# Gated attention and a squared-ReLU layer on one core: twelve units' loads, with and without waits in the SP queue

## The chip, the core and the metric

The kernel runs on one core of a Trainium2 chip. The core has five engines, each with its own instruction stream: TensorE (PE) for matmuls, VectorE (DVE), ScalarE (ACT), GpSimd (POOL), and SyncE (SP), which here does nothing but issue transfers. Engines wait for each other and for transfers through semaphores. Every engine works strictly in its written order: an instruction that waits holds up everything behind it on the same engine. The metric is device microseconds of one execution, and smaller is better.

## What is computed

```python
def _attn_ref(q, k, v, alpha):                       # batch 4, 8 heads, 768 tokens, 48 wide
    for t in range(S):
        state = alpha[:, :, t, :, None] * state + np.einsum('bhd,bhe->bhde', k[:, :, t], v[:, :, t])
        y[:, :, t] = np.einsum('bhd,bhde->bhe', q[:, :, t], state)

def _moe_ref(x, w_in, w_out):                        # 3072 tokens, 384 -> 2048 -> 384
    h = x @ w_in
    r = np.maximum(h, 0.0)
    g = r * r
    return (g @ w_out)
```

A gated linear attention runs over the tokens, and its output, with the heads side by side, goes through two dense layers with a squared ReLU between them.

## The kernel before

The work is cut into 12 units of 256 tokens: three steps along the sequence for each of four batch rows, all rows at one step first. A unit goes through these parts (the line numbers are those of the profile of before):

- **Loads.** Four transfers of 384 KB each, alpha, k, q and v, into one of four raw buffers (line 526, function `load`). Unit g uses buffer g modulo 4. Units 1 and 2 are loaded by POOL, all the others by SP.
- **Front.** From alpha come the decays: a product of pairs on DVE or POOL (lines 633, 635), logarithms on ACT (636, 675), a cumulative sum as a matmul on PE (642), exponentials on ACT (653, 655, 679). DVE multiplies them into k (709) and q (704). ACT or POOL casts v (700, 699).
- **Transposes.** From unit 3 on, two DMA transposes, a "pair" below, which SP issues (line 720), bring keys and queries into the buffer kqt.
- **Scores, output, state.** PE computes the scores (898), DVE masks them (909), PE computes the output of the attention and the new state (790, 801, 769), and ACT or DVE copies the output out as xbf (929, 931).
- **Dense layers.** xbf is transposed to xt, from unit 4 on by one DMA transpose that SP issues (line 950). PE multiplies with the first weight (1000), ACT or DVE applies the ReLU (1008, 1010), the square follows (1018, 1021, 1022), PE multiplies with the second weight (1040), ACT or DVE evicts to osb (1047, 1049), and SP issues the store (1056).

Nobody writes the engines' orders by hand. Every step is handed to `add` of a small planner (class `Program`) with an engine, a cost, a priority and what it reads and writes. `schedule` plays the whole program through with these costs and so fixes the order on each engine. `fill` puts dummy matmuls into the early holes of PE. `place` works out which semaphore waits each instruction needs, given what its engine has already waited for, and `emit` writes them. A step's dependencies are in `deps`, and `schedule` and `place` both read them.

Some dependencies do not come from data. `load` gives them through the argument `after`: the load that `AFTER` names (for every unit from 4 on the queries of the unit ahead, `(g - 1, "q")`, which for unit 4 are those of unit 3), and from unit 5 on a step of the unit ahead that `BEHIND` names: the logarithm `ln` for alpha, the multiplication `ekm` for k, the first transpose `tr0_` for q and v. These are called pacing waits here. In SP's queue, units interleave in this way from unit 5 on (the number is the unit): alpha 6, k 6, pair 5, transpose to xt 4, q 6, v 6, store, alpha 7, k 7, pair 6, transpose to xt 5, q 7, v 7, store, and so on.

Of the kernel before, what the change touches and what calls it, by code (L numbers as in the profile page):

```python
# [14 lines left out]
class Op:  # L15


    __slots__ = ("alts", "eng", "fn", "cost", "prio", "deps", "idx", "lag", "sem", "start", "end", "pos", "name",
                 "users", "ndeps", "mode", "ready", "land")

    def __init__(self, alts, prio, name):
        self.alts, self.prio, self.name = alts, prio, name
        self.eng = self.fn = self.cost = None
        self.deps = {}
        self.lag = 0
        self.sem = None
        self.users = []
        self.pos = None
        self.mode = ("F", "F")
        self.ready = 0.0  # L30
        self.start = self.end = self.land = None


class Program:
# [37 lines left out]
    def add(self, eng, fn, cost, prio, reads=(), writes=(), name="", dma=None, lag=0, after=(), mode=("F", "F"),  # L72
            alts=None):

        reads, writes = ([h for k in keys for h in ((k + (0,), k + (1,)) if len(k) == self.HALVED.get(k[0]) else (k,))]
                         for keys in (reads, writes))
        choices = {eng: (fn, cost)}
        if alts:
            choices.update(alts)
        if name in self.CHOSEN:  # L80
            choices = {self.CHOSEN[name]: choices[self.CHOSEN[name]]}
        op = Op(choices, prio + self.MOVED.get(name, 0), name)
        op.idx = len(self.ops)
        op.lag = lag
        op.mode = mode
        if dma is not None:
            if dma not in self.dma_sems:
                self.dma_sems[dma] = self.nc.alloc_semaphore("d_" + dma)
                self.dma_count[dma] = 0
            self.dma_count[dma] += 1  # L90
            op.sem = (dma, self.dma_count[dma])
        for o in after:
            op.deps[o] = True
        for k in reads:
            w = self.writer.get(k)
            if w is not None:
                op.deps[w] = True
            if k[0] == "ps":
                for r in self.readers.get(k, ()):
                    op.deps.setdefault(r, False)  # L100
        for k in writes:
            w = self.writer.get(k)
            if w is not None:
                op.deps[w] = True
            for r in self.readers.get(k, ()):
                if r is not op:
                    op.deps.setdefault(r, False)
        for k in reads:
            self.readers.setdefault(k, []).append(op)
        for k in writes:  # L110
            self.writer[k] = op
            self.readers[k] = []
        op.deps.pop(op, None)
        self.ops.append(op)
        return op
# [113 lines left out]
    def fill(self, make, sizes, until, after, cold):  # L229
# [23 lines left out]
            o.pos = i  # L253
        self.order["pe"] = new

    def place(self):
        known = {}
        snap = {}
        waits = {}
        seq = sorted(self.ops, key=lambda o: (o.start, o.idx))  # L260
        needed = set()

        def stream(o):
            return ("dma", o.sem[0]) if o.sem is not None else ("eng", o.eng)

        def place_of(o):
            return o.sem[1] if o.sem is not None else o.pos + 1

        for o in seq:
            kn = known.setdefault(o.eng, {})  # L270
            want = {}
            for d, raw in o.deps.items():
                if d.sem is None and d.eng == o.eng == "pe":
                    continue
                s, p = stream(d), place_of(d)
                if kn.get(s, 0) >= p:
                    continue
                if s not in want or place_of(want[s]) < p:
                    want[s] = d
            mine = []  # L280
            for d in sorted(want.values(), key=lambda d: -d.start):
                s, p = stream(d), place_of(d)
                if kn.get(s, 0) >= p:
                    continue
                mine.append(d)
                needed.add(d)
                for s2, p2 in snap[d].items():
                    if kn.get(s2, 0) < p2:
                        kn[s2] = p2
                if kn.get(s, 0) < p:  # L290
                    kn[s] = p
            waits[o] = mine
            snap[o] = dict(kn)
        self.waits = waits
        self.value = {}
        for ops in self.order.values():
            n = 0
            for o in ops:
                if o.sem is not None:
                    self.value[o] = 16 * o.sem[1]  # L300
                elif o in needed:
                    n += 1
                    self.value[o] = n
        self.needed = needed
# [34 lines left out]
def pe_ns(count, cols, at_once=1):  # L339
    return count * max(cols / 2.4 + 2.5, 25) / at_once  # L340
# [6 lines left out]
def dve_ns(n, rate=1.0):  # L347
    return 150 + n / 0.96 / rate
# [6 lines left out]
def bass_gla_recurrent__then__act_relu_squared_kernel(  # L355
# [24 lines left out]
    DENSE = {0: 19172, 1: 35978, 2: 46351, 3: 61182, 11: 160500}  # L380
    POOL_LOADS = {1: "akqv", 2: "akqv"}
    RATIO = 4
    NRAW, NQKS, NKQT, NPM, NV, NXT, NGT, NRR, NOSB = 4, 3, 3, 2, 4, 4, 2, 4, 2
    WS = 2
    LATE_STATE = (1, 2)
# [48 lines left out]
    pr = Program(nc)  # L434
# [18 lines left out]
    for i in range(2):  # L453
        add("dve", fill(LAF[i][:, :, :, D:64].rearrange("p j h d -> p (j h) d"), 0.0), 250, -1e6 - 10,
            writes=[("laf", i)])
        add("dve", fill(LAB[i][:, :, D:64], 0.0), 150, -1e6 + 20, writes=[("lab", i)])
    for i in range(NQKS):
        add("dve", fill(QKS[i][:, :, :, :, D:64].rearrange("p a j h d -> p (a j h) d"), 0.0), 500, -1e6 + 10,
            writes=[("qks", i, 0), ("qks", i, 1)])
# [7 lines left out]
    for part in (OWN[0:64, 0:H:2], OWN[64:128, 1:H:2]):  # L467
# [3 lines left out]
        writes=[("ident",)])  # L471
# [29 lines left out]
    load_op = {}  # L501
# [4 lines left out]
    def named(x):  # L506
        return next(o for o in pr.ops if o.name == x)

    BEHIND = {"a": "ln", "k": "ekm", "q": "tr0_", "v": "tr0_"}

    def load(g):
        b, i = units[g]
        t0 = i * T
        p0 = g * P
        r, la, qs, kt, pm, vb, x2 = (g % n for n in (NRAW, 2, NQKS, NKQT, NPM, NV, 2))
        first, last = i == 0, i == NST - 1
        sr, sw = 2 * b + i % 2, 2 * b + (i + 1) % 2

        for j, t, nm in ((0, alpha, "a"), (1, k, "k"), (2, q, "q"), (3, v, "v")):
            src = t[b, :, t0:t0 + T, :].rearrange("h (p j) d -> p h (j d)", j=2)  # L520
            dst, key = RAW[r][:, j], ("raw", r, j)
            ring, cost, gate = "sp", 600, AFTER.get((g, nm), AFTER.get(g))
            if nm in POOL_LOADS.get(g, ""):
                ring, cost = "pool", 930
            dst = dst.rearrange("p h j d -> p h (j d)")
            load_op[g, nm] = add(ring, lambda e, dst=dst, src=src: e.dma_start(dst, src), cost, (L_PRIO[g] + j if ring == "sp" else W_PRIO[2] + 10 * g + j if g > 1 else -6e5 + j),  # L526
                writes=[key], name=f"ld{nm}{g}", dma=f"{nm}{r}{ring}", lag=1230 if ring == "sp" else 1130,
                after=([load_op[gate]] if gate else []) + ([named(f"{BEHIND[nm]}{g - 1}")] if g >= 5 else []))

    def front_by_heads(g, p0):  # L530

# [96 lines left out]
    def decays_by_pair(g, p0, r, la, last):  # L628
# [11 lines left out]
        def m1(incl):  # L640
            def run(pe):
                ins = pe.matmul(psW[:, 0:HD], (LINC if incl else LSTR)[:], LAB[la][:, :, 0:D])  # L642
                if incl and not last:
                    for p in range(NPR):
                        ins = pe.matmul(psW[:, HD + 2 * p:HD + 2 * p + 2],
                                        LAB[la][:, 2 * p:2 * p + 2, :].rearrange("p h d -> p (h d)"), ONES2[:],
                                        start=(p == 0), stop=True, skip_group_check=True)
                return ins
            return run
# [7 lines left out]
        if not last:  # L657
# [5 lines left out]
                          dve_ns(HD))})  # L663
        if g < RATIO:
            add("pe", m1(False), pe_ns(1, HD), p0 + 530, reads=[("lab", la), ("lstr",)], writes=[("ps", "W")],
# [397 lines left out]
    for g in range(3, G):  # L1063
# [3 lines left out]
             ("wout", 1): (2, "k"), 3: ("wout", 0)}  # L1067
    AFTER.update({g: (g - 1, "q") for g in range(4, G)})
    load(0)
    load(1)  # L1070
    for w in range(WS):
        weight(0, w)
    load(2)
    for w in range(WS):
        weight(1, w)
    for st in ORDER:
        kind, g = st[0], int(st[1:])
# [10 lines left out]
        else:  # L1088
# [4 lines left out]
    pr.schedule()  # L1093
    pr.fill(lambda n: lambda pe: pe.matmul(psO[:, 0:n], ZERO[:, 0:128], ZERO[:, 0:n], skip_group_check=True),  # L1094
            ((512, 216, 420), (256, 109, 250)), min(o.start for o in pr.order["pe"] if o.name.startswith("s1_")), zero, 4600)
    pr.place()
    pr.emit()

# [27 lines left out]
```

## Time and profile before

| | us |
|---|---|
| median of 3 runs | 176.74 |
| lowest and highest run | 175.2, 177.66 |
| span of the profiled execution | 178.0 |
| PE busy in it | 168.6 |
| ACT busy in it | 119.4 |
| DVE busy in it | 120.3 |

The profile is one recorded execution. Its times are counted from the start of its span. A timeline row has the start, the length, the engine, the source line, the operation, the tile written and the tile read, and how many instructions were merged. In square brackets stands how long the engine was idle before the row and what ended that idle time. SP's rows (SPq) give how long SP itself was held by issuing, not how long the transfer took. The chain of waits has rows "DMA x<-y", whose length runs from the issue to the landing of a transfer.

### The profile page before, as it was taken

To read this page: it belongs to the slowest core of one execution; us is meant where nothing else is said; L and a number is where in the kernel's file an instruction comes from. 1 tells how busy PE (TensorE), PEld (TensorE's weight loads), DVE (VectorE), ACT (ScalarE), POOL (GpSimd) and SP (SyncE) were. 2 spreads that over 40 slices of the span, in tenths; PEclk is the share of its full clock that TensorE was granted. 3 is DMA by queue.
4 is the path that set the end of the run, shared out by engine and by line. 5 is a ranking of instruction groups with operands and counts; after the bars stand their busy time and mean duration, and the time that the engine had idled before them with its cause. 6 is when DMAs were issued, how large, how long until landed. Compare 5 with 4: busy or idle time off the path is not lost.

```text
span 178.0 us, 5087 instructions
## 1 busy us (share of the span) xinstructions
PE 168.6 (95%) x2232; PEld 130.6 (73%) x2234; DVE 120.3 (68%) x194; ACT 119.4 (67%) x214; POOL 24.2 (14%) x32
## 2 busy tenths in 40 slices
PE   7998998999996999999779999999999999999994
PEld 2655787856875778787558878878778787788773
DVE  5478579789885679984838876967958835423230
ACT  3838787867828588696388759859579554566450
POOL 3920951020304224200000000000000000000000
DMA  5999999979999799998999897999999692040022
GB/s 142 344 283 204 250 271 219 243 188 232 295 218 170 206 228 127 280 216 137 290 210 165 203 242 176 243 176 206 251 215 181 146 186 41 0 133 4 0 88 88
DMA packets 71030, 33.36 MB, mean 187 GB/s; under 512 B 67552, under 2 KB 67808, under 8 KB 71008
## 3 DMA queue, kind: packets, MB, share of 16 engines
q1 hardware_dynamic: 69024, 26.75, 67.6%
q0 software_dynamic: 1984, 6.29, 14.9%
q8 instruction: 17, 0.28, 0.6%
q14 instruction: 5, 0.04, 0.1%
HBM read 25.17 MB, written 4.72 MB: 168 GB/s over the span
## 4 chain that ended last, share of the span: by engine, by line
PE 74%; DMA 15%; ACT 5%; POOL 2%; DVE 1%; issue 1%; SPq 1%
PE psWH L1000 32%; PE psO L1040 29%; DMA raw<-in_v_dram 10%; DMA raw<-in_alpha_dram 5%; PE psZ L769 2%; PE psX L801 2%; POOL raw L526 2%; PE psX L898 2%; PE psX L790 2%; PE psX L970 1%; ACT rr L1008 1%; PE psZ L898 1%; PE psWH L642 1%; ACT vbf L700 1%; PE psZ L732 1%
## 5 line engine op out<-in xcount | busy, mean ns | idle before, releaser
L1000 PE MATMUL psWH<-xt,win 128*128 128x256 bf16 x576 | 73.9, 275 | 2.9 <-ACT rr L1008 1.8
L1000 PEld LDWEIGHTS psWH<-xt,win 128*128 128x128 bf16 x576 | 65.3, 145 | 8.1 <-ACT rr L1008 2.5
L1040 PE MATMUL psO<-wout,gt 128*128 128x384 bf16 x368 | 68.9, 326 | 1.9 <-ACT osb L1047 1.9
L1008 ACT ACTIVATE rr<-psWH 128x512 bf16<-128x512 f32 x85 | 50.1, 595 | 20.3 <-PE psWH L1000 18.6
L1040 PEld LDWEIGHTS psO<-wout,gt 128*128 128x128 bf16 x368 | 34.7, 98 | 20.5 <-ACT osb L1047 2.2
L1018 DVE TENSOR_TENSOR gt<-rr 128x1024 bf16<-128x1024 bf16 (+1 forms) x39 | 24.1, 622 | 25.3 <-ACT rr L1008 25.2
L909 DVE TENSOR_TENSOR pm<-psZ,caus 128x1024 bf16<-128x1024 f32 x12 | 14.6, 1219 | 2.4 <-PE psZ L898 2.4
L1022 ACT ACTIVATE gt<-rr 128x1024 bf16<-128x1024 bf16 (+1 forms) x18 | 15.2, 843 | 0.4
L909 DVE TENSOR_TENSOR pm<-psX,caus 128x1024 bf16<-128x1024 f32 x12 | 14.6, 1219 | 1.1 <-PE psZ L898 1.1
L929 ACT ACTIVATE xbf<-psX 128x768 bf16<-128x768 f32 x11 | 8.9, 809 | 7.1 <-PE psX L790 6.4
L700 ACT ACTIVATE vbf<-raw 128x768 bf16<-128x768 f32 x9 | 7.6, 841 | 8.6 <-DMA raw<-in_v_dram 8.6
L1047 ACT ACTIVATE osb<-psO 128x384 f32<-128x384 f32 x17 | 8.3, 489 | 5.2 <-PE psO L1040 4.8
L704 DVE TENSOR_TENSOR qks<-raw,eq 128x384 bf16<-128x384 f32 x18 | 9.8, 575 | 2.5 <-DMA raw<-in_q_dram 2.3
L1094 PE MATMUL psO<-zero 128*128 128x512 bf16 (+1 forms) x32 | 9.9, 437 | 1.5 <-DVE zero L447 1.3
L709 DVE TENSOR_TENSOR qks<-raw,ek 128x768 bf16<-128x768 f32 x11 | 10.5, 952 | 0.5 <-ACT ek L621 0.4
L1010 DVE TENSOR_SCALAR rr<-psWH 128x512 bf16<-128x512 f32 x11 | 7.6, 689 | 1.7 <-PE psWH L1000 1.2
L662 DVE TENSOR_TENSOR ek<-ek,raw 128x384 f32<-128x384 f32 x9 | 6.3, 705 | 1.4 <-ACT ek L653 1.4
L864 DVE TENSOR_TENSOR smd<-psZ,sbd 128x384 bf16<-128x384 f32 x8 | 4.4, 556 | 3.9 <-PE psX L790 3.9
L635 POOL TENSOR_TENSOR prd<-raw 128x384 f32<-128x384 f32 x4 | 4.0, 1002 | 19.5 <-DMA raw<-in_alpha_dram 19.5
L1094 PEld LDWEIGHTS psO<-zero 128*128 128x128 bf16 x34 | 3.2, 110 | 4.5 <-issue 1.9
L675 ACT ACTIVATE la<-raw 128x384 f32<-128x384 f32 x8 | 4.1, 518 | 3.4 <-DMA raw<-in_alpha_dram 3.2
L636 ACT ACTIVATE lab<-prd 128x384 bf16<-128x384 f32 x10 | 5.2, 521 | 1.7 <-DVE prd L633 1.7
(118 smaller groups left out, 171.7 us busy)
## 6 DMA issues: line engine op xcount, KB each, us to landing
out_dram<-osb SPq DMA_DIRECT2D x11, 384.0 KB, 4.1
raw<-in_alpha_dram SPq DMA_DIRECT2D x10, 384.0 KB, 3.6
raw<-in_k_dram SPq DMA_DIRECT2D x10, 384.0 KB, 5.3
raw<-in_q_dram SPq DMA_DIRECT2D x10, 384.0 KB, 3.9
raw<-in_v_dram SPq DMA_DIRECT2D x10, 384.0 KB, 5.2
win<-in_moe_w_in_dram POOLq DMA_DIRECT2D x2, 768.0 KB, 10.9
wout<-in_moe_w_out_dram POOLq DMA_DIRECT2D x2, 768.0 KB, 9.0
raw<-in_alpha_dram POOLq DMA_DIRECT2D x2, 384.0 KB, 4.6
```

Of the source, the lines that this page charges most:

```text
L700: name=f"vc{g}", alts={"act": (lambda e: e.activation(vout, vin, AF.Copy), act_ns(2 * HD))})
L704: add("dve", lambda e, j=j, dst=dst: e.tensor_tensor(dst, RAW[r][:, 2, :, j, :].rearrange("p (n x) d -> p n x d", x=2), EQ[la][:, j].rearr ...
L709: add("dve", lambda e, a=a, E=E: e.tensor_tensor(QKS[qs][:, a, :, :, 0:D], RAW[r][:, 1 + a].rearrange("p h j d -> p j h d"), E[la][:].rear ...
L909: add("dve", lambda e, hf=hf, psT=psT: e.tensor_tensor(PM[pm][:, hf].rearrange("p r n j t -> p (r n) (j t)"), psT[:, :, :].rearrange("p r ...
L929: add("act", lambda e: e.activation(XBF[x2][:], psX[:, :, 0:HD], AF.Copy), act_ns(2 * HD), p0 + 6100, reads=[("ps", "X", 0), ("ps", "X", 1 ...
L1000: ins = pe.matmul(psH[hb][:, i * T:(i + 1) * T], WIN[:, kk, hidden(fj)], mov, start=(kk == 0), stop=(kk == KT - 1))
L1008: add("act", lambda e, hb=hb, rr=rr: e.activation(rr, psH[hb], AF.Relu), act_ns(512), pu + 600, reads=[("ps", "H", hb)], writes=[("rr", rb ...
L1018: add("dve", lambda e, dst=dst, sq=sq: e.tensor_tensor(dst, sq, sq, ALU.mult), 148 + k * 267, pu + 1200, reads=[("rr", rb, h) for h in ran ...
L1022: "act": (lambda e, dst=dst, sq=sq: e.activation(dst, sq, AF.Square), act_ns(k * 512))})
L1040: ins = pe.matmul(psS, GT[gt][:, fj, j, :], WOUT[:, fj, :], start=(fj == 0), stop=(fj == FT - 1))
L1047: add("act", lambda e, j=j, psS=psS: e.activation(OSB[ob][:, j], psS, AF.Copy), act_ns(DM), ps_ + 700, reads=[keyS], writes=[("osb", ob, j ...
L1094: pr.fill(lambda n: lambda pe: pe.matmul(psO[:, 0:n], ZERO[:, 0:128], ZERO[:, 0:n], skip_group_check=True), ((512, 216, 420), (256, 109, 2 ...
```

## The change

Each load from unit 4 on remembers its pacing dependencies in a new attribute `pace`. The planner still reads them when it fixes the orders. Then `unpace` deletes them from `deps`, before `place` works out the waits. The orders on all five engines stay as they were. The waits on data stay: among them that a raw buffer has been read by the unit four before.

```diff
@@ class Op
     __slots__ = ("alts", "eng", "fn", "cost", "prio", "deps", "idx", "lag", "sem", "start", "end", "pos", "name",
-                 "users", "ndeps", "mode", "ready", "land")
+                 "users", "ndeps", "mode", "ready", "land", "pace")
...
+        self.pace = ()
...
@@ class Program
+    def unpace(self):
+
+        for o in self.ops:
+            for d in o.pace:
+                del o.deps[d]
...
+    FREE = 4
...
@@ def load(g)
+            pace = ([load_op[gate]] if gate else []) + ([named(f"{BEHIND[nm]}{g - 1}")] if g >= 5 else [])
             load_op[g, nm] = add(ring, lambda e, dst=dst, src=src: e.dma_start(dst, src), cost, (L_PRIO[g] + j if ring == "sp" else W_PRIO[2] + 10 * g + j if g > 1 else -6e5 + j),
-                writes=[key], name=f"ld{nm}{g}", dma=f"{nm}{r}{ring}", lag=1230 if ring == "sp" else 1130,
-                after=([load_op[gate]] if gate else []) + ([named(f"{BEHIND[nm]}{g - 1}")] if g >= 5 else []))
+                writes=[key], name=f"ld{nm}{g}", dma=f"{nm}{r}{ring}", lag=1230 if ring == "sp" else 1130, after=pace)
+            if g >= FREE:
+                load_op[g, nm].pace = pace
...
     pr.fill(lambda n: lambda pe: pe.matmul(psO[:, 0:n], ZERO[:, 0:128], ZERO[:, 0:n], skip_group_check=True),
             ((512, 216, 420), (256, 109, 250)), min(o.start for o in pr.order["pe"] if o.name.startswith("s1_")), zero, 4600)
+    pr.unpace()
     pr.place()
     pr.emit()
```

## The prediction

> **What bounds the kernel now.** I read the busy times first, then TensorE (PE) by stretches, then the instructions on either side of each PE gap, and last the queue of SP, which is where the change acts.
>
> ```profile
> PE 168.6 (95%) x2232; PEld 130.6 (73%) x2234; DVE 120.3 (68%) x194; ACT 119.4 (67%) x214; POOL 24.2 (14%) x32
> ```
> ```profile
> 36.00:90.00 54.00, 50.17 (x716) 38.28 (x715) 43.15 (x65) 36.91 (x73) 9.44 (x8) 1.00 0.97 217
> 90.00:174.00 84.00, 83.93 (x1058) 66.99 (x1059) 51.08 (x79) 56.64 (x97) 0.00 (x0) 1.00 0.70 148
> ```
>
> In the second fence the columns are length, busy time of PE, PEld, DVE, ACT and POOL, granted clock, DMA share and GB/s. From 90 us to 174 us PE lacks 0.07 us of being busy throughout, at clock 1.00: nothing that a load does can shorten that stretch. Between 36 and 90 us PE is idle for 54.00 - 50.17 = 3.83 us. The first load whose waits go is issued at 38.81 us (below), so these 3.83 us are all that the change can win. The gaps, by PE's timeline:
>
> ```profile
> 52.61 0.82 PE L1000 MATMUL psWH<-xt,win 128*128 128x256 bf16 x6
> 55.00 0.88 PE L1000 MATMUL psWH<-xt,win 128*128 128x256 bf16 x6 [1.57 <-ACT rr L1008]
> 64.41 0.87 PE L1000 MATMUL psWH<-xt,win 128*128 128x256 bf16 x6 [0.27 <-ACT rr L1008]
> 86.52 1.47 PE L1000 MATMUL psWH<-xt,win 128*128 128x256 bf16 x12
> 89.92 2.29 PE L1040 MATMUL psO<-wout,gt 128*128 128x384 bf16 x13 [1.93 <-ACT osb L1047]
> ```
>
> Three gaps, 1.57 + 0.27 + 1.93 = 3.77 us, each ended by an eviction on ACT. ACT's own timeline tells why the eviction was late, and the chain of waits (start, length) tells how long the transfer behind it took from issue to landing:
>
> ```profile
> 53.94 0.52 ACT L675 ACTIVATE la<-raw 128x384 f32<-128x384 f32 x1 [2.57 <-DMA raw<-in_alpha_dram]
> 54.37 0.58 ACT L1008 ACTIVATE rr<-psWH 128x512 bf16<-128x512 f32 x1
> 63.03 0.84 ACT L700 ACTIVATE vbf<-raw 128x768 bf16<-128x768 f32 x1 [0.86 <-DMA raw<-in_v_dram]
> 88.65 0.84 ACT L700 ACTIVATE vbf<-raw 128x768 bf16<-128x768 f32 x1 [2.58 <-DMA raw<-in_v_dram]
> 89.40 0.47 ACT L1047 ACTIVATE osb<-psO 128x384 f32<-128x384 f32 x1
> ```
> ```profile
> 0.80 3.49 DMA raw<-in_alpha_dram
> ...
> 48.01 5.91 DMA raw<-in_alpha_dram
> ...
> 57.05 5.96 DMA raw<-in_v_dram
> ...
> 82.66 5.97 DMA raw<-in_v_dram
> ```
>
> ACT works in its written order: it stands before an instruction that reads a load (alpha of unit 5, v of unit 5, v of unit 7), and the eviction that PE needs is queued behind it. So three late loads make the three gaps, and the question is how much earlier each of the three can be issued.
>
> **SP's queue, and what the change takes out of it.** In the built programs the five engines have the same sequences before and after; 24 waits vanish, all on loads in SP's queue, and none is added. What they cost now:
>
> ```profile
> SPq L526 <- DMA raw<-in_q_dram: 17.6, 7, 4.0
> ```
> ```profile
> 34.34 1.15 SPq L526 DMA_DIRECT2D raw<-in_v_dram  x1
> 38.81 0.37 SPq L526 DMA_DIRECT2D raw<-in_alpha_dram  x1
> ...
> 41.51 1.65 SPq L526 DMA_DIRECT2D raw<-in_v_dram  x1
> 43.21 1.18 SPq L1056 DMA_DIRECT2D out_dram<-osb  x1
> 44.43 3.47 SPq L720 DMA_TRANSPOSE kqt<-qks  x2
> 48.01 1.35 SPq L526 DMA_DIRECT2D raw<-in_alpha_dram  x1
> ...
> 50.07 5.13 SPq L720 DMA_TRANSPOSE kqt<-qks  x2
> ...
> 56.56 0.44 SPq L526 DMA_DIRECT2D raw<-in_q_dram  x1
> ...
> 61.91 0.37 SPq L526 DMA_DIRECT2D raw<-in_alpha_dram  x1
> ...
> 63.04 4.32 SPq L720 DMA_TRANSPOSE kqt<-qks  x2
> ...
> 69.34 0.50 SPq L526 DMA_DIRECT2D raw<-in_q_dram  x1
> ...
> 73.28 0.37 SPq L526 DMA_DIRECT2D raw<-in_alpha_dram  x1
> ...
> 74.46 5.42 SPq L720 DMA_TRANSPOSE kqt<-qks  x2
> 79.93 2.06 SPq L950 DMA_TRANSPOSE xt<-xbf  x1
> ...
> 82.66 0.58 SPq L526 DMA_DIRECT2D raw<-in_v_dram  x1
> ...
> 140.29 3.07 SPq L720 DMA_TRANSPOSE kqt<-qks  x2
> ```
>
> Columns: start, time in SP's queue, what is issued. Seven alpha loads wait 17.6 us for the queries of the unit ahead. That is not the gain. In this order each pair of transposes (line 720), the store and the transpose to xt (line 950) keep their own waits for DVE and ACT, and the next loads stand behind them. I go through the three late loads.
>
> *Alpha of unit 5 (gap of 1.57 us).* Unit 4's alpha can be issued when v of unit 3 is out of SP's hands, 34.34 + 1.15 = 35.49, instead of 38.81: 3.3 us earlier, and k, q and v of unit 4 with it. What follows has these inputs:
>
> ```profile
> 41.13 0.48 ACT L1047 ACTIVATE osb<-psO 128x384 f32<-128x384 f32 x1
> ```
> ```profile
> 41.89 0.56 DVE L704 TENSOR_TENSOR qks<-raw,eq 128x384 bf16<-128x384 f32 x1
> ...
> 61.98 1.03 DVE L704 TENSOR_TENSOR qks<-raw,eq 128x384 bf16<-128x384 f32 x2 [1.21 <-DMA raw<-in_q_dram]
> ...
> 66.49 0.96 DVE L931 CAST xbf<-psX 128x768 bf16<-128x768 f32 x1 [1.22 <-PE psX L790]
> ```
>
> The store's data are ready at 41.61, yet SP reaches it at 43.21, being in the issue of v until 43.16. The transposes' data are ready at 42.45, yet they start at 44.43. Freed of that, the store starts at 41.61, the transposes at 41.61 + 1.18 + 0.04 = 42.83, and alpha of unit 5, which follows them at once, 1.6 us earlier than 48.01. I take 1.6. The ends are 0 (should the transfers ahead still fill the queue) and 3.3 (should the pair's 3.47 us shrink as well). The load then lands 1.6 earlier than 53.92, the eviction at 54.37 comes at 52.8 and ends at 53.4, and PE, whose block before it ends at 52.61 + 0.82 = 53.43, runs on: **-1.57 us**.
>
> *v of unit 5 (gap of 0.27 us).* Before it stand the pair at 50.07, a store and q at 56.56. The pair took 5.13 us in SP's queue where a pair with no load ahead of it took 3.07 (at 140.29), so its end is set by the two loads ahead of it, and those now come 1.6 us earlier. The store's eviction moves with ACT's 1.6. I take 1.5 us for q and v. PE also asks 1.57 us earlier, so the gap stays as it is: **0**. What is late next is again v.
>
> *v of unit 7 (gap of 1.93 us).* Alpha of unit 6 leaves at about 56.4 and not at 61.91, which fills part of the hole in the DMA engines here (share 0.59, last column but one):
>
> ```profile
> 60.00:64.00 4.00, 4.00 (x59) 3.22 (x58) 2.79 (x4) 2.41 (x5) 0.00 (x0) 1.00 0.59 154
> ```
>
> It brings the pair at 63.04 forward by 1.5 (its queries end DVE's wait at 61.98). But q of unit 6 stands behind the transpose of xbf, which is ready at 66.49 + 0.96 = 67.45 and is set by PE. So from there SP's work comes 1.5 to 1.6 us earlier, with PE, and not more. The alpha of unit 7 then loses its own wait: it goes at about 70.4, 2.9 us earlier than 73.28. That helps only as far as the transfers ahead of the pair at 74.46 are not already back to back. The pair's 5.42 us in the queue against 3.07 says that they nearly are. I give 0.4 of those 2.35 us. Line 950 at 79.93 follows the pair at once and v at 82.66 follows line 950, so v of unit 7 comes 1.5 + 0.4 = 1.9 us earlier, while PE asks for it 1.57 earlier: **-0.33 us**, and a gap of about 1.6 stays. Ends: +1.57 (v gains nothing, and the first gap's gain is lost here) and -1.93 (v comes 3.5 us earlier).
>
> *Units 8 to 11.* PE has no gap there, so no gain. Nor should a new one open: loads and PE have both come forward by about 1.9, and this is the longest that ACT waits for one after 90 us, without a stop of PE:
>
> ```profile
> 128.52 0.84 ACT L700 ACTIVATE vbf<-raw 128x768 bf16<-128x768 f32 x1 [1.11 <-DMA raw<-in_v_dram]
> ```
>
> Issuing costs nothing new: the loads, their sizes and their places are the same, and SP is not on PE's path except through them. Four raw buffers keep the loads apart from their readers; those waits refer to the unit four before and are long met.
>
> **Sum.** -1.57 + 0 - 0.33 = -1.9 us on a span of 178.0 us, so 176.1 us in a profile like this one. The page gives the profiled execution's span alone. It is 1.26 us above the median of 176.74 and above the highest of the three runs (177.66), so the gaps of an ordinary run may be somewhat smaller or the recording adds a little. Taking the same 1.9 us from the median gives 174.8, and I round towards the deeper end of the third term: **174.6 us**.
>
> **Rivals.** *All gaps go.* If v of unit 7 comes 3.5 us earlier, PE is gap-free and the time is 176.74 - 3.83 = 172.9 us. For it: the pair's and line 950's stay in SP's queue (5.42 + 2.06 us) has much queueing in it. Against it: the same bytes go in the same order, and q of unit 6 still waits for PE. Chance 0.24.
>
> *Landings stretch and give it back.* A load on an empty queue landed in 3.49 us (at 0.80), and the three late ones took 5.91 to 5.97 among others, 2.4 us more. With q, v, the store, alpha and k of two units queued together, v of unit 7 could take another 1.9 us; the third gap then grows to 1.93 + 1.57 = 3.5, and the time is 176.7. Against it: these loads stand behind v and not ahead of it. Chance 0.12. The Trainium skill, "DMA: Bandwidth & Descriptors", section "Latency and other measured facts", gives an HBM latency of 0.2 us on average and 2 us at high load, which speaks against filling the queue earlier. By it each landing would take up to 1.8 us longer (an estimate from that page), and nearly the whole sum would go. The trace cannot separate such a latency from plain queueing.
>
> *Slower: loads crowd the pairs of transposes.* If the earlier loads run beside the pair and not before it, every pair of units 6 to 10 would again lose what the pair at 74.46 loses against that at 140.29, 5.42 - 3.07 = 2.35 us. ACT stood a wait of 1.11 us without a gap on PE, so about 1.25 us would show in each, 5 x 1.25 = 6.2, less the 1.9 won: +4.3 us, 181.0 us. It decides the sign from about 1.5 us lost per pair. Against it: every pair has the same transfers ahead of it in SP's order as now, and a wait taken out of one queue lets nothing overtake. Chance 0.10. The same page's section "Queues, rings and completion order" has the descriptors of a queue taken up in ring order on each DMA engine, which speaks against this rival; no row here shows single engines.
>
> That the change does nothing at all is excluded by the built queue, and that it moves issues but no gap is the second rival.
>
> **How the numbers follow.** Forecast 0.54, all gaps 0.24, given back 0.12, crowding 0.10. The forecast's own range, from its bounds, is 173.0 to 176.0. The range from 172.6 to 176.8 takes in the first two rivals and leaves out crowding and the edges, less than 0.2. A measurement of this kernel tells about 2% from no change, here below 173.2 or above 180.3. Faster than that: 0.17 of the 0.24, since 172.9 lies just beyond it, and 0.13 of the forecast, together 0.30. Slower: 0.10, the crowding. Within: 0.60.
>
> **What would show it.** In the changed profile SP waits no more for q at the loads' line. Unit 4's alpha leaves within 0.1 us of v of unit 3, and unit 6's near 56.4. PE has no gap near 53.4, a small one near 62.6 and one of about 1.6 us near 86.4, again behind v, so that 1.9 us of idle PE time are left there in place of 3.83. Wrong would be: the first gap still there (then alpha of unit 5 is not bound by issue), the last one gone (first rival), the last one at 3.5 us (second), or new gaps after 90 us before the scores (line 898) with pairs that stay in the queue longer than now (third).

## The result, and the profile after

The changed kernel has a median of 175.50 us in 19 runs (174.65 to 177.3), the kernel before one of 177.66 us in its 19 runs beside it (175.2 to 180.88). The ratio of the two is 0.9939 (95% interval 0.991 to 0.9967): about 1.1 us or 0.6% faster. The ratio leaves out executions that lie more than 1.5% above the fastest of their own kernel, which is why it is closer to 1 than the ratio of these medians. The forecast was 174.6 us from 176.74, 1.2% faster. The direction was right, and so was the likeliest of the three outcomes, within 2%, but the forecast size was twice the measured one.

The recorded execution after has a span of 174.0 us and a time of 175.72 us, so 1.7 us lie around the span. PE's busy time on the page, then the stretches from 36 to 90 and from 90 to 170 us (length, busy PE, PEld, DVE, ACT, POOL, clock, DMA share, GB/s), then the only gap that PE's timeline has after 36 us, and ACT's instruction behind it:

```profile
PE 168.1 (97%) x2234; PEld 130.0 (75%) x2234; DVE 119.1 (68%) x194; ACT 119.6 (69%) x214; POOL 24.0 (14%) x32
```
```profile
36.00:90.00 54.00, 53.24 (x795) 40.72 (x794) 43.13 (x67) 39.78 (x77) 8.51 (x7) 1.00 1.01 224
...
90.00:170.00 80.00, 79.94 (x977) 64.25 (x976) 49.69 (x77) 53.41 (x92) 0.00 (x0) 1.00 0.69 147
```
```profile
62.48 0.88 PE L1010 MATMUL psWH<-xt,win 128*128 128x256 bf16 x6 [0.71 <-ACT rr L1018]
```
```profile
61.10 0.84 ACT L710 ACTIVATE vbf<-raw 128x768 bf16<-128x768 f32 x1 [1.31 <-DMA raw<-in_v_dram]
```

The reader should see that of 3.83 us of idle PE time between 36 and 90 us 0.76 are left, nearly all of it one gap behind v of unit 5. The gaps near 53 and near 88 us are gone. In SP's queue (line 535 is the loads' line now, 730 the pair's, 960 that of the transpose to xt):

```profile
33.35 1.15 SPq L535 DMA_DIRECT2D raw<-in_v_dram  x1
34.55 1.11 SPq L535 DMA_DIRECT2D raw<-in_alpha_dram  x1
...
45.96 1.26 SPq L535 DMA_DIRECT2D raw<-in_alpha_dram  x1
...
55.92 2.80 SPq L535 DMA_DIRECT2D raw<-in_alpha_dram  x1
...
70.09 0.44 SPq L535 DMA_DIRECT2D raw<-in_alpha_dram  x1
...
72.53 3.96 SPq L730 DMA_TRANSPOSE kqt<-qks  x2
76.68 1.81 SPq L960 DMA_TRANSPOSE xt<-xbf  x1
...
79.16 0.58 SPq L535 DMA_DIRECT2D raw<-in_v_dram  x1
```

Alpha of unit 4 follows v of unit 3 after 0.05 us, alpha of units 6 and 7 no longer wait. A row to remember is the pair of unit 6: it stays 3.96 us in SP's queue, where it stayed 5.42 us before.

### The profile page after: what moved, and what is told of

Its sections match the earlier page's. It is cut to its first block, busy times and chain, and to the rows that moved or that the text cites. A ratio compares the mean times of both kernels' runs of the same rounds, so it can differ in the third digit from the quotient of the medians.

```text
span 174.0 us, 5086 instructions
## 1 busy us (share of the span) xinstructions
PE 168.1 (97%) x2234; PEld 130.0 (75%) x2234; DVE 119.1 (68%) x194; ACT 119.6 (69%) x214; POOL 24.0 (14%) x32
## 4 chain that ended last, share of the span: by engine, by line
PE 78%; DMA 14%; POOL 3%; ACT 2%; DVE 1%; issue 1%; SPq 1%
PE psWH L1010 33%; PE psO L1050 33%; DMA win<-in_moe_w_in_dram 5%; DMA raw<-in_alpha_dram 5%; DMA raw<-in_v_dram 4%; POOL raw L535 2%; PE psX L811 2%; PE psZ L779 2%; PE psX L908 2%; PE psX L800 2%; PE psX L980 2%; PE psZ L908 1%; PE psWH L652 1%; ACT rr L1018 1%; POOL prd L645 1%
## 5 line engine op out<-in xcount | busy, mean ns | idle before, releaser
L1059 DVE COPY osb<-psO 128x384 f32<-128x384 f32 x6 | 3.3, 557 | 4.6 <-PE psO L1050 4.6
```

## The experiments

All kernels below compute the whole result. A kernel that chooses which loads lose their waits is the changed one with this edit:

```diff
-    FREE = 4
+    FREED = (4,)
...
-            if g >= FREE:
+            if g in FREED:
```

**The paced kernel, recorded four more times.** With `FREED = ()` no wait goes, and the program is the one before.

> No load loses its waits: the same program as before, recorded once more. Theory A (one execution differs from the next mainly in how long PE stands at the late loads between 36 and 90 us): span minus PE's idle time in 36 to 90 us comes out at about 174.2 us again (178.0 - 3.83), whatever the span is, and the times spread over some 175 to 181 us. Theory B (the executions differ in something that has nothing to do with the loads, the start for instance): PE's idle time in 36 to 90 us is about 3.8 us again, whatever the span. Ratio to before 1.00 by both.

> No load loses its waits: the kernel before, recorded once more at full clock. Theory G (an execution lies above another by the gaps that PE has at late loads, and the recorded one of before was one of the long ones): its time less its span is 1.7 us again, and its span less all of PE's idle time after 36 us is about 174.1 us (178.0 - 3.83 - 0.07), whatever the span. If its time is below 177 us, PE's idle time after 36 us is under 1.2 us. Theory B (the first term of the prediction is typical): the gap near 53 us of about 1.5 us is there again.

> The kernel before, third record. Theory G: PE's gaps near 53, 63 and 88 us differ again from 1.57, 0.27 and 1.93 us; span less PE's idle time after 36 us is 173.5 to 174.5 us whatever the span; ACT's wait for alpha of unit 5 follows the landing (4.1 us in one record, 5.9 in the other), not the issue near 48 us. Theory B: the three gaps are there with about the same sizes.

> The kernel before, fourth record; the same as for the third.

The first of these has a ratio of 1.0027 (0.9961 to 1.0094). Two of its 12 runs took 283.0 and 945.93 us, and its recorded execution is the former, at a granted clock of 0.563, so its profile says nothing here. The second has 0.9988 (0.9935 to 1.0041). The other three records stand beside the one that the prediction was made from, in the next table. The gaps are those of PE's timeline, idle is what PE lacks of 54.00 us between 36 and 90 us, and a further 0.06 or 0.07 us are idle after 90 us. The last two columns are taken from the transfers behind the gap near 88 us: how long the pair of unit 6 stays in SP's queue, and how long v of unit 7 takes from issue to landing.

| record of before | time us | span us | gaps near 53, 63, 88 us | idle | span less all idle after 36 us | pair of unit 6, us | v of unit 7, us |
|---|---|---|---|---|---|---|---|
| that of the prediction | not given | 178.0 | 1.57, 0.27, 1.93 | 3.83 | 174.1 | 5.42 | 5.97 |
| paced_again | 176.87 | 175.1 | none, 1.09, none | 1.09 | 174.0 | 4.60 | 4.59 |
| paced_look3 | 178.39 | 176.7 | none, 0.65, 2.33 | 3.06 | 173.6 | 5.75 | 5.73 |
| paced_look4 | 178.6 | 176.8 | none, 0.73, 2.37 | 3.10 | 173.6 | 5.55 | 6.06 |

PE's, ACT's and SP's rows of paced_again come first, then of paced_look3 PE's two gaps, ACT's rows, SP's rows and, from the chain of waits, the landing of v of unit 7:

```profile
63.71 0.88 PE L1010 MATMUL psWH<-xt,win 128*128 128x256 bf16 x6 [1.09 <-ACT rr L1018]
```
```profile
52.41 0.52 ACT L685 ACTIVATE la<-raw 128x384 f32<-128x384 f32 x1 [0.77 <-DMA raw<-in_alpha_dram]
```
```profile
48.33 0.53 SPq L535 DMA_DIRECT2D raw<-in_alpha_dram  x1
...
73.69 4.60 SPq L730 DMA_TRANSPOSE kqt<-qks  x2
```
```profile
62.72 0.87 PE L1010 MATMUL psWH<-xt,win 128*128 128x256 bf16 x6 [0.65 <-ACT rr L1018]
88.56 1.64 PE L1050 MATMUL psO<-wout,gt 128*128 128x384 bf16 x9 [2.33 <-ACT osb L1057]
```
```profile
51.87 0.53 ACT L685 ACTIVATE la<-raw 128x384 f32<-128x384 f32 x1 [1.08 <-DMA raw<-in_alpha_dram]
...
87.29 0.84 ACT L710 ACTIVATE vbf<-raw 128x768 bf16<-128x768 f32 x1 [2.98 <-DMA raw<-in_v_dram]
88.03 0.47 ACT L1057 ACTIVATE osb<-psO 128x384 f32<-128x384 f32 x1
```
```profile
46.77 1.34 SPq L535 DMA_DIRECT2D raw<-in_alpha_dram  x1
...
71.96 0.37 SPq L535 DMA_DIRECT2D raw<-in_alpha_dram  x1
...
73.09 5.75 SPq L730 DMA_TRANSPOSE kqt<-qks  x2
...
81.54 0.58 SPq L535 DMA_DIRECT2D raw<-in_v_dram  x1
```
```profile
81.54 5.73 DMA raw<-in_v_dram
```

Theory G holds: span less idle is 173.6 to 174.1 us in all four, so one execution of this kernel stands above another by PE's gaps, to within 0.5 us. Theory B is out: the gap near 53 us, which the prediction took for the first of three, is in one record of four. (It is also absent from the four records below in which alpha of unit 4 keeps its wait.) It does not follow the issue of alpha of unit 5. That load went out at 48.01 in the first record and at 48.33 in paced_again, and ACT read it at 53.94 and at 52.41: a landing of 5.9 us against 4.1. The gap near 88 us is in three records of four. Where it is, two things are longer: the pair of unit 6 stays 5.42, 5.75 and 5.55 us in SP's queue (4.60 us where the gap is not), and v of unit 7, issued behind it, then takes 5.97, 5.73 and 6.06 us to land (4.59 us where the gap is not).

**Unit 4 alone**, `FREED = (4,)`: one wait goes.

> Only unit 4's loads lose their wait (one wait: alpha of unit 4 for the queries of unit 3). Theory A (the prediction's first term): alpha of unit 4 leaves within 0.1 us of v of unit 3, alpha of unit 5 leaves 1.6 us earlier than 48.0 and the gap of PE near 53.4 is gone; the later ones stay. That is 1.57 us against the profile of before, and most of the 0.6% that the whole change brings. Rival C (the later units' waits bring it): the gap near 53.4 stays and the ratio is 1.00 within its interval.

Ratio 0.9972 (0.9911 to 1.0034). The gap near 53 us is absent, but it mostly is without the edit too. The pair of unit 6 and the gap near 88 us, from SP's and from PE's timeline, then the landing of v of unit 7:

```profile
72.48 5.84 SPq L730 DMA_TRANSPOSE kqt<-qks  x2
```
```profile
86.26 2.77 PE L1050 MATMUL psO<-wout,gt 128*128 128x384 bf16 x16 [0.37 <-ACT osb L1057]
```
```profile
80.32 4.64 DMA raw<-in_v_dram
```

This edit leaves the long stay as it was and a small gap: with v landing after 4.64 us, the long stay alone does not bring the 1.9 to 2.4 us. Its runs reach 181.07 us, and the interval does not tell its effect from none.

**Units 5 to 7**, `FREED = (5, 6, 7)`.

> Only units 5, 6 and 7 lose their waits. Theory A: the gap near 53.4 stays, since alpha of unit 4 still waits for q of unit 3; the gap near 88 shrinks or goes, because alpha and k of units 6 and 7 no longer wait for the queries ahead and the pair of unit 6 stays about 1.5 us less in SP's queue. Ratio between 0.995 and 1.00. Rival C: most of the gain is here, ratio 0.994, spread as narrow as with the whole change.

Ratio 0.9962 (0.9916 to 1.0008); lowest and highest run 174.93 and 177.16. The pair of unit 6, and PE running through 88 us with no idle time in brackets:

```profile
73.52 3.37 SPq L730 DMA_TRANSPOSE kqt<-qks  x2
```
```profile
85.58 1.48 PE L1010 MATMUL psWH<-xt,win 128*128 128x256 bf16 x12
86.89 2.76 PE L1050 MATMUL psO<-wout,gt 128*128 128x384 bf16 x16
```

The gap near 88 us is absent without these waits, whether unit 4 waits or not, and the spread is as narrow as with the whole change, as rival C has it. The gap near 53 us is absent although unit 4 waits, against what was expected.

**Units 8 to 11**, `FREED = (8, 9, 10, 11)`, and the reverse, `FREED = (4, 5, 6, 7)`, twice.

> Only units 8 to 11 lose their waits. Theory A: PE has no gap after 90 us in the profile of before, so nothing changes: ratio 1.00 within its interval, the same spread of times as before, gaps before 90 us as before. Rival D (in other executions of before PE also stands after 90 us, and this is what the whole change removes): ratio clearly below 1, 0.994 or so, and fewer high times.

> Units 4 to 7 lose their waits, units 8 to 11 keep them. Theory A (nothing to gain after 90 us): times and spread as with the whole change, PE's idle time from 90 to 170 us 0.07 us. Rival D' (once the early gaps are gone, the waits of units 8 to 11 can hold a pair of transposes and with it the transpose to xt, as in the recorded run with alpha and k of unit 7 freed, where a gap of 1.57 us stood at 134.6 us): a gap of 0.3 to 2 us between 120 and 140 us in the profile, and some times above 177.5 us, median 0.3 to 1 us above the whole change.

> Units 4 to 7 without their waits, 8 to 11 with them, second record. Theory A: no gap of PE from 90 to 170 us beyond 0.07 us. Rival D': a gap of 0.3 to 2 us between 120 and 140 us.

Units 8 to 11 alone: 0.9984 (0.9925 to 1.0042), and the gap near 88 us stood at 2.45 us in the record (pair of unit 6: 5.94 us, landing of v of unit 7: 5.85 us). Units 4 to 7 without 8 to 11: 0.9948 (0.9902 to 0.9993), beside 0.9914 (0.9875 to 0.9952) for the whole change on the same chip. In both its records PE has 79.94 us of 80.00 from 90 to 170 us. So no record shows a gap that units 8 to 11 bring there. The median is 0.30 us above that of the whole change (175.87 and 175.57 us), the lower end of what rival D' has, and that difference lies within the intervals.

**The whole change again**, on that chip.

> The changed kernel once more, on one chip with the others of this set. Theory G: PE's idle time after 36 us is under 1 us, span about 174, no run above 177.5 us but for one with a low clock; ratio to before between 0.984 and 0.997, by how long the gaps of before are on this chip.

Ratio 0.9914 (0.9875 to 0.9952), span 173.3 us, one run of the 12 above 177.5 us (180.12), and no idle PE time at all from 36 to 90 us, so the last gap comes and goes as well. The pair of unit 6 stays 3.90 us in the queue.

**Alpha and k of unit 7 alone**, and **all but these two**:

```diff
+    FREED = ((7, "a"), (7, "k"))
...
+            if (g, nm) in FREED:
```

> Only alpha and k of unit 7 lose their waits (for q of unit 6, and for steps of unit 6's front). Theory A': the last gap before 90 us is set by these two. With the waits they go out just ahead of the pair of unit 6 and the pair then stays 5.4 to 5.9 us in SP's queue; without, they go 1.3 us or more earlier, the pair stays under 4 us and v of unit 7 comes in time. Then the gap near 88 us is under 0.5 us, nearly no run lies above 177.5 us, and the ratio is that of units 5 to 7 together, about 0.996. Rival E (the shift adds up over units 5, 6 and 7): the gap near 88 us is still 1 us or more in most executions and the times spread up to 180 us as before.

> All loads of units 4 to 11 lose their waits except alpha and k of unit 7. Theory A': most of the gain is lost again; the pair of unit 6 stays more than 5 us in SP's queue, a gap of 0.4 to 2.5 us stands near 86 us, and times above 177.5 us come back. Rival E: like the whole change, ratio 0.994 and no times above 177.5 us.

Freed alone: ratio 0.9959 (0.9904 to 1.0014). The pair stays 4.17 us and the gap near 88 us is gone, as theory A' has it, but five of ten runs are above 177.5 us (up to 178.19), and the record has other gaps: 1.28 us near 62 us, and one of 1.57 us at 134.6 us. For the latter, PE's timeline and SP's:

```profile
136.15 0.88 PE L1010 MATMUL psWH<-xt,win 128*128 128x256 bf16 x6 [1.57 <-DMA xt<-xbf]
```
```profile
118.73 0.57 SPq L535 DMA_DIRECT2D raw<-in_q_dram  x1
...
124.59 0.37 SPq L535 DMA_DIRECT2D raw<-in_alpha_dram  x1
...
125.72 5.71 SPq L730 DMA_TRANSPOSE kqt<-qks  x2
...
132.09 1.25 SPq L960 DMA_TRANSPOSE xt<-xbf  x1
```

It looks like the same thing some rounds later: q of unit 10 takes 5.8 us to land, and alpha of unit 11 waits for it for 4.6 us after SP is done with v of unit 10. Alpha goes out 1.1 us ahead of a pair, the pair stays 5.71 us, and the transpose to xt behind it is late. Kept alone, all others freed: 0.9872 (0.9788 to 0.9956) in four runs. The pair stays 4.70 us and the gap near 88 us is absent in the record, so in it these two waits alone do not bring the gap back once the units ahead have lost theirs, against theory A'. But two of the four runs are above 177.5 us (177.6 and 178.66), which rival E rules out and theory A' does not. Neither theory fits both edits, and which waits of units 5 to 7 matter stays open. These two ran on a chip on which the kernel before had a median of 178.97 us, so their ratios compare with each other and with the first two of the next group only.

**The casts of v later on ACT**, once with all waits and twice without them. After the orders are fixed, `later` lets a step change places with the next one in ACT's order:

```diff
+    LATER = ("vc5", "vc7")
...
+    for name in LATER:
+        pr.later(name)
```

> All waits as before; on ACT the casts of v of units 5 and 7 change places with the instruction behind each (a ReLU eviction, and the eviction to osb). Theory A (PE stands only because ACT, in its written order, waits for v ahead of the eviction that PE needs): with the loads as late as before, the gaps near 64 and 88 us go, unless v is needed itself for the state soon after; ratio 0.995 to 0.997 and a narrow spread. Rival F (PE waits for something else that is late with v, such as the scores' pair): the gap near 88 us stays.

> The whole change, and the casts of v of units 5 and 7 one place later on ACT. Theory A: the gap of 0.71 us near 62.5 us, the last one, shrinks or goes; PE's idle time from 36 to 90 us falls from 0.76 us to under 0.3; ratio 0.991 to 0.994, at best 0.5 us below the changed kernel. Rival F: the gap stays and so does the time.

> The whole change with the casts of v of units 5 and 7 one place later on ACT, beside the changed kernel on the same chip. If this is a better version, its median is 0.2 to 0.7 us below that of the changed kernel and no run is above 176.5 us. If the gap of 0.71 us near 62.5 us is only passed on to the output of the attention, the two medians agree within 0.2 us.

With all waits: 0.9841 (0.9766 to 0.9916) in four runs, one of them at 179.15 us. ACT now evicts ahead of the cast (first fence), PE goes on without idle time near 86 us (second), and PE's only gap from 36 to 90 us is another (third):

```profile
84.47 0.49 ACT L1067 ACTIVATE osb<-psO 128x384 f32<-128x384 f32 x1 [0.65 <-PE psO L1060]
84.86 0.84 ACT L720 ACTIVATE vbf<-raw 128x768 bf16<-128x768 f32 x1
```
```profile
85.58 2.76 PE L1060 MATMUL psO<-wout,gt 128*128 128x384 bf16 x16
```
```profile
63.08 0.19 PE L810 MATMUL psX<-sbd,kqt 64*128 64x48 bf16 x1 [0.56 <-DVE pm L929]
```

The pair of unit 6 stays 5.42 us here, as long as in the first record of before, and yet there is no gap near 88 us. That does not yet show what the change of places is worth, because v of unit 7 landed after 4.92 us, at 84.55. With the cast ahead of the eviction, PE's block would have started 1.27 us behind the start of the cast, as in paced_look3 (87.29 to 88.56), so at about 85.82 in place of 85.58: some 0.25 us later (an estimate from these rows). An execution with a landing as slow as 5.7 us was not recorded with this edit. Near 63 us the wait is passed on to the masks of the scores, which stand behind DVE's wait of 1.23 us for q. Without the waits: 0.9844 (0.9791 to 0.9898), on the chip of the row above, and 0.9928 (0.9881 to 0.9974) beside the whole change's 0.9914, medians 175.78 and 175.57 us. In these two records 0.16 us and nothing are idle between 36 and 90 us. The two remedies do not add up, and no version that ran beside the changed kernel beats it.

## Why the prediction was right, and where it was wrong

*PE is the bound, and only its gaps between 36 and 90 us can go.* Right. Span less idle stays at 173.2 to 174.1 us through the records of before and after (after: 174.0 - 0.76 - 0.06 = 173.2; 174.6 in the record of units 5 to 7 freed), and no gap opened after 90 us in the two records of the whole change. The two recorded spans differ by 4.0 us, of which 3.1 are gaps. The other 0.9 us are no gain of the change: v of unit 3, which keeps its waits, already goes out 0.99 us earlier (34.34 and 33.35).

*First term, -1.57 us for alpha of unit 5.* This step failed. The issue did move, from 13.7 us behind v of unit 3 (34.34 to 48.01) to 12.6 (33.35 to 45.96), by 1.1 us and not 1.6. But the gap was no property of the kernel. It is in one of four records of before, where that load took 5.9 us to land, and the prediction read "three late loads" out of one execution as if each were late every time. So 1.57 of the forecast's 1.9 us were taken from a gap that most executions do not have.

*Second term, 0 for v of unit 5.* Right in kind. That gap has 0.27 to 1.09 us in the records of before and 0.71 or nothing after.

*Third term, -0.33 us for v of unit 7.* Mis-sized, and it is where the gain lies. The step "I give 0.4 of those 2.35 us" held that the transfers ahead of the pair of unit 6 were nearly back to back. The pair's stay fell by 1.5 us, to 3.96 and 3.90, and lies between 3.4 and 4.3 us in every record with units 5 to 7 freed. The prediction itself named the quantity to look at, the stay against 3.07 us at an empty queue, and then took a sixth of it. A second step failed beside it: the sum moved the landing of v by as much as its issue, and so put a change of the time between them, 5.97 us before, at nothing. It took 4.42 us after. PE's block of 12 matmuls ahead of the gap and ACT's cast of v, after:

```profile
84.59 1.47 PE L1010 MATMUL psWH<-xt,win 128*128 128x256 bf16 x12
```
```profile
84.04 0.83 ACT L710 ACTIVATE vbf<-raw 128x768 bf16<-128x768 f32 x1
```

Against the start of that block, v of unit 7 was issued 3.86 us ahead before (82.66 and 86.52) and 5.43 us ahead after (79.16 and 84.59). So between these two records v won 1.57 us by its issue and 1.55 us by its landing, 3.1 us in all, where the term had 0.33, and ACT no longer waits for it. The landing tells the records apart. Of the six with the waits of units 5 to 7 and the casts in their old place, four have a landing of 5.7 to 6.1 us and a gap of 1.9 to 2.5 us, and two have 4.6 us and a gap of 0.37 us or none. In the seven without these waits (two of them with the casts moved) the landing is 4.4 to 4.7 us, and the gap is absent from all.

*The base of the sum.* "Taking the same 1.9 us from the median" failed too. Time less span is 1.7 to 1.8 us in the records that have both, so the recorded execution of before took about 179.7 us, 3 us above the median shown and not 1.26. Its 3.77 us of gaps were those of a long execution. An execution like paced_again, at 176.87 us and close to that median, has 1.09 us to lose, which is of the size of the ratio of 0.9939. That the two medians of 19 runs differ by 2.16 us, near the forecast's 2.14, is luck: most of the forecast was the gap near 53 us, and what the records lose is the gap near 88 us.

*The rivals.* "All gaps go" came true for PE in one of two records (free_again), but the change is worth 1.1 us and not 3.8, for the reason just given. "Landings stretch" did not come true for v. These are the page's rows on issues (median us from issue to landing last), before and then after:

```profile
raw<-in_alpha_dram SPq DMA_DIRECT2D x10, 384.0 KB, 3.6
...
raw<-in_v_dram SPq DMA_DIRECT2D x10, 384.0 KB, 5.2
```
```profile
raw<-in_alpha_dram SPq DMA_DIRECT2D x10, 384.0 KB, 5.2
...
raw<-in_v_dram SPq DMA_DIRECT2D x10, 384.0 KB, 4.5
```

Alpha, issued earlier, takes 1.6 us longer from issue to landing, and v 0.7 us less. With v the load that PE's gaps hang on, the rule on latency at high load, which the prediction took from "DMA: Bandwidth & Descriptors" in the Trainium skill, took nothing back here. "Crowding" did not come true: the pairs of units 5 to 10 stay 3.1 to 4.0 us in the queue, where they stayed 4.2 to 5.4 us before.

What stays open is why the landing of one and the same load differs by almost 2 us between executions and why v of unit 7 lands sooner without the waits, and how much the waits of units 8 to 11 cost where early ones are gone. The record with alpha and k of unit 7 freed has a gap of 1.57 us behind such a wait, the two with units 4 to 7 freed have none.

## What to carry to other kernels

Before pricing a gap, ask whether the recorded execution is an ordinary one: compare its time, not its span, with the median, and record the kernel twice. A wait in an in-order issuing queue need not be paid where it waits. Here it pushed loads right in front of a pair of transposes. That pair then stayed 4.6 to 5.9 us in the queue, against 3.4 to 4.3 us without the waits, and the load behind it came late. How late was decided as much by that load's own landing, so look at issue and landing apart. And an instruction that reads a late load should not stand ahead of an eviction that the busiest engine needs: each of the three gaps ended with such an eviction. What moving it by one place is worth where the load is really late, no record here shows.

## What the runs showed that was not expected

A gap on PE may cost more than its length. In the record of units 8 to 11 freed (180.0 us), the gap of 2.45 us was followed by a stretch at half clock, from 88.75 to 92.17 us. First PE's timeline, then the windows around it, where the last column but two is the granted clock:

```profile
88.47 4.45 PE L1050 MATMUL psO<-wout,gt 128*128 128x384 bf16 x16 [2.45 <-ACT osb L1057]
```
```profile
88.00:89.00 1.00, 0.53 (x3) 0.36 (x4) 1.00 (x2) 1.00 (x4) 0.00 (x0) 0.88 0.75 208
89.00:90.00 1.00, 1.00 (x5) 0.46 (x3) 0.96 (x2) 0.97 (x2) 0.00 (x0) 0.50 0.46 86
90.00:91.00 1.00, 1.00 (x5) 0.46 (x3) 0.00 (x0) 1.00 (x3) 0.00 (x0) 0.50 1.07 151
91.00:92.00 1.00, 1.00 (x4) 0.46 (x3) 0.00 (x0) 0.30 (x1) 0.00 (x0) 0.50 0.89 133
```

The 16 matmuls took 4.45 us against 2.76 to 2.77 elsewhere, so if the gap brought this, it cost 2.45 + 1.68 us. Gaps of 2.33 and 2.37 us in two other records were not followed by such a stretch, and no second record has a gap as long, so the cause is not shown. The Trainium skill, "TensorE: Matmul & The Clock Gate", Part 1, has the clock fall to half after an idle window of about 3.4 us and return after about 3.4 us of work. The return agrees, with some 3.4 us at 0.50 here. The fall came after less idle time than that page says, and here the measurement decides.
